# A Fourier and SwiGLU block: seven second products per weight group in place of eight, another modulation sum and a finer handing out

## The chip, the cores and the metric

One core of a Trainium2 chip. The metric is device time in microseconds (us) of one execution; lower is better. The engines are TensorE (PE, matmuls, with its weight loads PEld), VectorE (DVE), ScalarE (ACT), GpSimd (POOL) and the DMA queues, which SyncE (SP) and POOL feed here.

## The reference

The shapes are x: (1, 2048, 512), w1 and w3: (512, 1792), w2: (1792, 512), w_mod: (512, 3072), all fp32.

```
mod = (silu(c) @ w_mod).reshape(1, 6, 1, 512)
sa, ca, ga, sb, cb, gb = mod
h = layernorm(x) * (1 + ca) + sa
x = x + ga * fourier(h)              # real part of a 2-D DFT, by four DFT matrices
h = layernorm(x) * (1 + cb) + sb
x = x + gb * ((silu(h @ w1) * (h @ w3)) @ w2)
```

## The kernel before

**Precision.** Every fp32 operand is split in a high part (a rounded copy made on ACT) and a low part (the difference, made on DVE). A product is three matmul passes: high-high, high-low, low-high (`PASSES`, `product` L98). One matmul is 128 x 128 against 128 x 512.

**Stages.** Hidden-dimension DFT (to about 88 us in the profile), sequence DFT (to 262), then the SwiGLU part. The sequence stage also works off a queue of background steps: the columns of w_mod for ga, sb, cb and gb (`mod_columns` L344, multiply by silu(c) and sum along the row), and the second layernorm (`ln2` L817).

**SwiGLU.** The 2048 tokens are four chunks t = 0 to 3 of 512 columns, in pairs (0, 2) and (1, 3). The 1792 features are seven groups g of 256. Groups 0 and 1 of pair 0 are multiplied plainly: `up_block` for w1 and w3 (24 matmuls), then `down_unit` for w2. The order there is up(0,0), up(1,0), eight down units of chunk 0, then up(0,2), up(1,2), with up(g, t).

All else runs in twelve **items** (g, pair), counted 0 to 11: five of pair 0, then seven of pair 1, in `items`. In an item the first products are by Strassen's scheme (Winograd's form): seven products in place of eight block products for w1, called a1 to a7, and seven for w3, b1 to b7 (`factor` L1239). Each is a **unit** of six matmuls. ACT or DVE reads a unit's PSUM bank out, after which a later unit adds onto the same bank. DVE forms v = silu(gate) * up in `result` and v is split into hf. The second products, by w2, are units of six matmuls too, written **y**: eight an item, two chunks times four blocks of output columns, alternating on banks 6 and 7. ACT copies a bank into a tile y, scaled by gb (L335), and POOL adds two of them at a time onto `sums` in DRAM by an accumulating DMA. Items 10 and 11 (g = 5, 6 of pair 1) add on DVE onto reloaded sums `xr` instead. The y units of an item run inside the next item.

**Order.** The order on PE is written out by hand, as a string per item (last lines of `folded`): `-b7 a1 a2 -b4 -b3` (the leading minus is the last item's), then `a6 a5 y a7 y y a4 y a3 y b1 y b2 y b6 b5 y`. Item 5, the **turning** item (0, 1), has its own string. The weights of the next item, and this item's w2, are split by **jobs** (`weight_jobs` L1164: highs, sums, lows, highs and lows of the sums; `plain_jobs` for w2). Jobs and background steps are taken from their queues by `advance` after each unit or block, as long as a credit of DVE and ACT time lasts; each step declares its cost, and a `PAUSE` ends a call. `behind(n, f)` records f after n more units. Every engine runs its instructions in recorded order.

Of the kernel before, what the change touches and what calls it, by code (L numbers as in the profile page):

```python
# [42 lines left out]
def folded(nc, pools, c, cp, wmr, wmc, x, xt, ctr, cti, wdr, wdi, w1, w3, w2, out):  # L43
# [300 lines left out]
    def mod_columns(v, dst):  # L344
        w = {}

        def fetch(i):
            w[i] = take(F32, "wmc")
            nc.sync.dma_start(w[i], wmc[v, i])

        def scale(i):
            times(w[i], w[i], sc_row[0][:, 0, :].unsqueeze(1).to_broadcast([P, 2, N]))

        def total(i):
            r1 = small.tile([P, 32], F32, name=f"r1_{v}_{i}", tag="r1")
            nc.vector.tensor_reduce(
                out=r1,
                in_=flat(w[i]).rearrange("p (a b) -> p a b", b=32),
                axis=AX.X,
                op=OP.add,  # L360
            )
            nc.vector.tensor_reduce(
                out=dst[:, 2 * i : 2 * i + 2],
                in_=r1.rearrange("p (a b) -> p a b", b=16),
                axis=AX.X,
                op=OP.add,
            )
            give(w[i])
# [12 lines left out]
        background.extend([PAUSE] * 2)  # L381
        for i in range(2):
            step(background, 0, lambda i=i: scale(i), 1.2)
            step(background, 0, lambda i=i: total(i), 1.3)
        step(background, 0, end, 0.1)


# [685 lines left out]
            later[n - 1] = later.pop(n)  # L1073


    def up_block(g, t, q, w):
        if q == 0 and w == "w1":
            drain(lambda: ("h2", t, 1) in done)
        to = bank(turn[0] % 4)
        turn[0] += 1  # L1080
        for d in range(ND):
            at = slice(d * P, (d + 1) * P)
            product(
                to,
                [u[:, q, at] for u in wuse[w, g]],
                [u[t, d // 2][:, d % 2, :] for u in (h2h, h2l)],
                d == 0,
                d == ND - 1,
            )
        if t == PAIRS[0][1] and q == 1:  # L1090
# [117 lines left out]
    TO = {1: 0, 6: 0, 7: 0, 4: 0, 2: 1, 5: 2, 3: 2}  # L1208
    state, vs = {}, {}

    def right(pair, n):
        t0, t1 = PAIRS[pair]
        if n in (1, 2, 3):
            at = {1: (t0, 0), 2: (t0, 1), 3: (t1, 1)}[n]
            return h2h[at], h2l[at]
        at = pair, {5: 1, 6: 2, 7: 3, 4: 4}[n]
        return th[at], tl[at]

    def result(i, w, q, k, src):
# [6 lines left out]
        times(v, v, src)  # L1226

        def highs():
            hf[g, PAIRS[pair][k], q] = take(F32R, "hf")
# [5 lines left out]

        behind(1, highs)
        behind(2, lows)

    def factor(i, w, n):  # L1239
        g, pair = items[i]  # L1240
# [36 lines left out]
        if n == 3:  # L1277
            for x in wuse.pop(key).values():
                give(x)
            behind(1, lambda: give(st["x"]))  # L1280
            if w == "w3":
                for x in vs.pop(i):
                    behind(3, lambda x=x: give(x))


    loads.extend((n, m) for n in range(len(steps)) for m in range(2))
# [292 lines left out]
    def down(g, pair, t, d, key):  # L1579
        drain(lambda: (key, "l") in done, jobs)  # L1580
        delayed()
        down_unit(g, pair, t, d, key)
        beside(1.36, USED["own" if pair == 1 and g >= NG - 2 else "y"])

    for w in ("w1", "w3"):
# [25 lines left out]
    def other_operands():  # L1611
# [6 lines left out]
                give(h.pop((0, n)))  # L1618
        sum_parts(jobs, *sums_of.pop())

    def unit(kind, i, n):
        g, pair = items[i]
        more = i + 1 < len(items)
# [14 lines left out]
        if (kind, n) == ("a", 3) and more:  # L1638
            load_w(("w3", *items[i + 1]))
            weight_jobs(i + 1, "w1")  # L1640
        if (kind, n) == ("b", 2):
            plain_jobs(("w2", g, pair))
        if (kind, n) == ("b", 3):
            if i + 2 == turning:
                drain(lambda: ("xc", 3) in done)
# [7 lines left out]
            for t in PAIRS[pair]:  # L1653
                seconds.extend((g, pair, t, d, ("w2", g, pair)) for d in range(ND))
        beside(1.36, FACTOR[kind][n])

    weight_jobs(0, "w3")
# [822 lines left out]
```

## Time and profile before

| | us |
|---|---|
| median of 3 runs | 708.48 (707.67 to 708.64) |
| the profiled execution | 708.46 |
| its span, first to last instruction | 706.7 |
| up and down stage, 262 to 320: PE, DVE, ACT busy | 55.72, 43.34, 32.69 of 58 |
| items 0 to 4, 320 to 470: PE, DVE, ACT busy | 148.43, 130.02, 105.25 of 150 |
| item 5, 470 to 500: PE, DVE, ACT busy | 30.00, 20.47, 20.51 of 30 |
| the end, 650 to 706.7: PE, DVE, ACT busy | 48.55, 31.80, 15.02 of 56.7 |

A matmul's duration in the profile (0.39) is longer than its share of PE, since matmuls overlap; the distance between two starts is what a matmul costs. The same holds for ACT and DVE instructions that follow each other without a wait. A wait is shown in square brackets with the engine and the tile that ended it.

### The profile page before, as it was taken

The page shows a single profiled execution, that of the slowest core. Times are in us where ns is not written, and L with a number is a line of the kernel's source. Part 1 is how long each engine was busy: PE and PEld are TensorE (multiplying, and loading weights), DVE is VectorE, ACT ScalarE, POOL GpSimd, SP SyncE. Part 2 cuts the span into 40 slices and gives each one's busy share as a digit, 9 for nine tenths or more (in the row PEclk, how much of TensorE's full clock was granted, in tenths as well). Part 3 has the DMA queues.
Part 4 walks back from the last instruction along what each step waited for, and adds up shares of the span by engine and source line. Part 5 has one row for each costly group of instructions (what it writes and reads, how often), then busy time and mean ns, then how long its engine had stood idle before and what let it go on. Part 6 is the DMA issues. An engine that isn't in the chain of part 4 may idle for free.

```text
span 706.7 us, 8912 instructions
## 1 busy us (share of the span) xinstructions
PE 686.3 (97%) x3152; PEld 564.7 (80%) x3152; DVE 548.3 (78%) x877; ACT 430.8 (61%) x709; POOL 119.4 (17%) x141
## 2 busy tenths in 40 slices
PE   7999999999999999899999999999999999999995
PEld 4898888888888888687888788787788888888784
DVE  5999679997999978579987886896865556664763
ACT  4998865545454655745677676867665565656420
POOL 1320253542524000200100101011010100101000
PEclk9999999999999999999999999999999999999998
DMA  8730299796678521522868558376763847537403
GB/s 266 211 120 1 77 373 328 251 307 229 207 283 287 168 86 41 92 58 64 209 114 199 89 130 153 61 156 137 239 136 73 180 62 175 111 69 162 137 0 124
DMA packets 38100, 108.93 MB, mean 154 GB/s; under 512 B 4896, under 2 KB 5152, under 8 KB 38048
## 3 DMA queue, kind: packets, MB, share of 16 engines
q0 software_dynamic: 12352, 43.00, 29.3%
q1 hardware_dynamic: 25264, 63.98, 27.5%
q10 hardware_dynamic: 432, 1.31, 0.5%
q8 instruction: 26, 0.43, 0.3%
q14 instruction: 26, 0.21, 0.1%
HBM read 76.81 MB, written 33.55 MB: 156 GB/s over the span
## 4 chain that ended last, share of the span: by engine, by line
PE 81%; DVE 7%; ACT 6%; issue 2%; DMA 2%; SPq 1%; ACTq 0%; DVEq 0%
PE bank L100 52%; PE bank L750 25%; PE bank L559 2%; PE bank L598 1%; DMA wmr<-in_wmr 1%; ACT xc L894 1%; PE bank L576 1%; DVE xc L96 1%; SPq L231 1%; ACT hf L87 1%; ACT y L335 1%; DVE v L96 0%; DVE hl L90 0%; ACT hm L501 0%; DMA w<-in_wdi 0%
## 5 line engine op out<-in xcount | busy, mean ns | idle before, releaser
L100 PE MATMUL bank<-hf,w2h 128*128 128x512 f32 (+1 forms) x452 | 140.9, 391 | 0.3
L1146 POOL DMA_DIRECT2D sum<-y x48 | 41.0, 855 | 390.1 <-ACT y L335 373.0
L100 PEld LDWEIGHTS bank<-hf,w2h 128*128 128x128 f32 x452 | 84.3, 188 | 22.1 <-DVE hf L90 3.4
L100 PE MATMUL bank<-hf,w2l 128*128 128x512 f32 (+1 forms) x226 | 87.6, 388 | 0.0
L87 ACT ACTIVATE hf<-v 128x512 fp32r<-128x512 f32 x56 | 35.3, 630 | 67.3 <-DVE v L96 62.7
L335 ACT ACTIVATE y<-bank,gb 128x512 f32<-128x512 f32 x96 | 64.9, 682 | 18.6 <-PE bank L100 18.3
L93 DVE TENSOR_TENSOR v<-bank,x 128x512 f32<-128x512 f32 x36 | 24.7, 685 | 34.9 <-PE bank L100 34.8
L750 PE MATMUL bank<-bh,us 128*128 128x512 f32 x128 | 49.9, 390 | 0.0
L93 DVE TENSOR_TENSOR x<-bank,x 128x512 f32<-128x512 f32 x36 | 24.7, 687 | 32.4 <-PE bank L100 28.7
L750 PE MATMUL bank<-bh,ul 128*128 128x512 f32 x128 | 49.8, 389 | 0.0
L750 PE MATMUL bank<-d,us 128*128 128x512 f32 x128 | 49.8, 389 | 0.0
L750 PE MATMUL bank<-d,uh 128*128 128x512 f32 x128 | 49.8, 389 | 0.0
L750 PE MATMUL bank<-l,us 128*128 128x512 f32 x128 | 49.8, 389 | 0.0
L750 PE MATMUL bank<-l,uh 128*128 128x512 f32 x128 | 49.8, 389 | 0.0
L100 PEld LDWEIGHTS bank<-hf,w2l 128*128 128x128 f32 x226 | 42.4, 188 | 8.4
L90 DVE TENSOR_TENSOR hf<-v,hf 128x512 fp32r<-128x512 f32 x56 | 38.5, 687 | 12.2 <-ACT hf L87 12.1
L170 POOL DMA_INDIRECT re<-in_ctr,mirror x32 | 35.8, 1117 | 66.2 <-DVE ul L90 39.5
L1224 ACT ACTIVATE v<-v 128x512 f32<-128x512 f32 x36 | 22.8, 632 | 38.8 <-DVE v L93 38.8
L87 ACT ACTIVATE x<-bank 128x512 f32<-128x512 f32 x72 | 41.4, 586 | 7.2 <-PE bank L100 6.5
L170 POOL DMA_INDIRECT im<-in_cti,mirror x32 | 32.7, 1023 | 35.3 <-PE bank L750 10.0
L100 PE MATMUL bank<-h2h,w1h 128*128 128x512 f32 x80 | 31.8, 397 | 1.5 <-ACT h2h L87 1.5
L100 PE MATMUL bank<-h2l,w1h 128*128 128x512 f32 x80 | 31.9, 399 | 0.8 <-DVE h2l L90 0.8
(246 smaller groups left out, 1775.2 us busy)
## 6 DMA issues: line engine op xcount, KB each, us to landing
sum<-y POOLq DMA_DIRECT2D x48, 512.0 KB, 5.6
w<-in_w SPq DMA_DIRECT2D x42, 512.0 KB, 4.5
re<-in_ctr SPq DMA_DIRECT2D x32, 256.0 KB, 5.0
im<-in_cti SPq DMA_DIRECT2D x32, 256.0 KB, 5.0
wmc<-in_wmc SPq DMA_DIRECT2D x8, 512.0 KB, 6.3
xr<-in_xt SPq DMA_DIRECT2D x8, 512.0 KB, 7.6
sum<-xr SPq DMA_DIRECT2D x8, 512.0 KB, 6.2
x<-in_x SPq DMA_DIRECT2D x11, 256.0 KB, 4.8
```

The costliest lines, as they stand in the source:

```text
L87: nc.scalar.activation(dst, src, AF.Copy, scale=scale)
L90: nc.vector.tensor_tensor(out=dst, in0=a, in1=b, op=OP.subtract)
L93: nc.vector.tensor_tensor(out=dst, in0=a, in1=b, op=OP.add)
L96: nc.vector.tensor_tensor(out=dst, in0=a, in1=b, op=OP.mult)
L100: nc.tensor.matmul(acc, lhs[a], rhs[b], start=first and n == 0, stop=last and n == len(PASSES) - 1, skip_group_check=more,)
L170: nc.gpsimd.indirect_dma_start(dst, None, rows, bass.IndirectOffsetOnAxis(ap=at, axis=0))
L231: queue.dma_start(raw_w[dt][q * 64 : (q + 1) * 64, m, :], w[i][par::2, q])
L335: nc.scalar.activation(dst, src, AF.Identity, scale=by)
L559: nc.tensor.matmul(halves(hb[k])[:, m, :], sides((hh, hl)[a][k])[:, dt, m, :], wu[dt][:, b, m, :], start=False, stop=dt % 2 == 1 and n == ...
L750: nc.tensor.matmul(acc[what, e], lhs, rhs, start=begin and i == 0, stop=(end or (turn and what == "x")) and i == len(terms) - 1, skip_grou ...
L1146: nc.gpsimd.dma_start(sums[t, d // 2], y, accum_op=OP.add)
L1224: behind(k != 0 or q == 0, lambda: nc.scalar.activation(v, src, AF.Silu))
```

## The change

**Second products.** For items 5 to 9, (0, 1) to (4, 1), listed in `SEVEN`, w2 is multiplied by seven products (`seven_unit`) in the order 2 5 3 1 6 7 4. Each is one unit: three matmuls on bank 6 and three on bank 7, half the output columns each. Products 2, 5 and 1 start the two banks anew; 3 adds onto 5, and 6, 7, 4 onto 1. After each, ACT copies both banks into a y tile and POOL accumulates it, seven times an item. `seven_parts` forms the seven right-hand operands from v (four differences on DVE and seven splits), `seven_jobs` the sums of w2 and their splits. The y strings of items 6 to 10 lose one y, and no two y follow each other directly.

**Weights.** In these items the job for the next w3 is queued at b6 and no longer at b3, except in item 5, where w3 stays at b3 and the w2 job moves from b2 to b3.

**Modulation.** The product and row sum of a w_mod tile (one multiply and two reductions of up to 1024 columns) become eight multiply-and-sum instructions of 128 columns and one small reduction. The declared cost is 2 x 0.9 for a tile, before 1.2 + 1.3.

**Handing out.** `up_block` runs in two halves, and `advance` is called after each with 1.36, before once with 2.72.

```diff
+        def total(i, b):
+            sums, junk = parts[i], w[i][:, b, :]
+            for n in range(ND):
+                nc.vector.scalar_tensor_tensor(
+                    junk[:, cols(n)],
+                    junk[:, cols(n)],
+                    1.0,
+                    sc_row[0][:, 0, cols(n)],
+                    op0=OP.mult,
+                    op1=OP.mult,
+                    accum_out=sums[:, b, n : n + 1],
+                )
...
-            step(background, 0, lambda i=i: scale(i), 1.2)
-            step(background, 0, lambda i=i: total(i), 1.3)
+            for b in range(2):
+                step(background, 0, lambda i=i, b=b: total(i, b), 0.9)
...
+    def seven_parts(i, q, k):
...
+        if (q, k) != (0, 1):
+            n = {(0, 0): 1, (1, 0): 2, (1, 1): 3}[q, k]
+            behind(1, lambda: high(n, v[q, k]))
+            behind(2, lambda: low(n, v[q, k]))
+            return
+        t1, t2, t3, t4 = v[0, 0], v[1, 1], v[0, 1], v[1, 0]
+        behind(1, lambda: minus(t1, v[0, 1], v[0, 0]))
+        behind(2, lambda: high(5, t1))
+        behind(2, lambda: minus(t3, v[1, 1], v[0, 1]))
+        behind(3, lambda: low(5, t1))
+        behind(3, lambda: minus(t2, v[1, 1], t1))
...
+    def seven_jobs(key):
...
+        step(jobs, 1, highs, 0.0, 1.0)
+        step(jobs, 1, totals, 1.4)
+        step(jobs, 1, lows, 1.2)
+        step(jobs, 1, sum_highs, 0.0, 1.0)
+        step(jobs, 1, sum_lows, 1.2)
+
+    def seven_unit(g, pair, n, key):
...
+        for e, to in enumerate(banks7):
+            at = int(LEFT7[n][1]) * HALF + e * P
+            product(
+                to,
+                [flat(wuse[key][x])[:, at : at + P] for x in names],
+                [u[:, b, :] for b in range(2)],
+                new,
+                True,
+                not new,
+            )
+            d = 2 * which + e
+            copy_by(y[:, e, :], to, gb[:, d : d + 1])
+        give(u)
+        nc.gpsimd.dma_start(sums[t, which], y, accum_op=OP.add)
+        behind(4, lambda: give(y))
+        if n == ORDER7[-1]:
...
+            if g == NG - 3:
+                for t in PAIRS[pair]:
+                    load_sums(t)
...
-                up_block(g, t, q, w)
-                beside(2.72, USED[w])
+                for part in range(2):
+                    up_block(g, t, q, w, part)
+                    beside(1.36, USED[w] if part else (0.0, 0.0))
...
-        if (kind, n) == ("b", 2):
-            plain_jobs(("w2", g, pair))
+        if (kind, n) == ("b", 3 if i == turning else 2):
+            (seven_jobs if (g, pair) in SEVEN else plain_jobs)(("w2", g, pair))
...
-            if more:
+            if more and not early_w3(i):
                 weight_jobs(i + 1, "w3")
...
+        if (kind, n) == ("b", 6) and more and early_w3(i):
+            weight_jobs(i + 1, "w3")
...
+        if i and items[i - 1] in SEVEN:
+            body = "a6 a5 a7 y a4 y a3 y b1 y b2 y b6 y b5 y"
```

Where the order moves, first on ACT, in the down units between up(1,0) and up(0,2). The tiles xc are chunk 2 after its layernorm, scaled in place; h2h is its high part, which up(0,2) reads; y are the copies of the eight units. Before:

```order
L335 ACTIVATE y_381_2743<-bank4_382_2744,gb_152 128x512
L335 ACTIVATE y_381_2743<-bank5_383_2759,gb_152 128x512
L335 ACTIVATE y_384_2769<-bank6_385_2770,gb_152 128x512
L894 ACTIVATE xc_348_2564<-xc_348_2564,sb_150,cb1_151 128x512 x2
L335 ACTIVATE y_384_2769<-bank7_386_2780,gb_152 128x512
L335 ACTIVATE y_387_2790<-bank4_388_2791,gb_152 128x512
L894 ACTIVATE xc_360_2611<-xc_360_2611,sb_150,cb1_151 128x512 x2
L335 ACTIVATE y_387_2790<-bank5_389_2801,gb_152 128x512
L335 ACTIVATE y_390_2810<-bank6_391_2811,gb_152 128x512
L87 ACTIVATE h2h_392_2819<-xc_348_2564 128x1024
L335 ACTIVATE y_390_2810<-bank7_394_2823,gb_152 128x512
L87 ACTIVATE h2h_395_2832<-xc_360_2611 128x1024
```

And in the changed kernel, at the same place:

```order
L897 ACTIVATE xc_342_2546<-xc_342_2546,sb_150,cb1_151 128x512 x2
L87 ACTIVATE hf_379_2797<-v_377_2777 128x512
L897 ACTIVATE xc_350_2616<-xc_350_2616,sb_150,cb1_151 128x512 x2
L335 ACTIVATE y_381_2804<-bank4_382_2805,gb_152 128x512
L335 ACTIVATE y_381_2804<-bank5_383_2813,gb_152 128x512
L87 ACTIVATE h2h_384_2822<-xc_342_2546 128x1024
L335 ACTIVATE y_386_2826<-bank6_387_2827,gb_152 128x512
L87 ACTIVATE h2h_388_2835<-xc_350_2616 128x1024
L335 ACTIVATE y_386_2826<-bank7_390_2839,gb_152 128x512
L335 ACTIVATE y_391_2849<-bank4_392_2850,gb_152 128x512
```

The scalings moved ahead of the first y copy, and both h2h from behind the seventh and eighth y copy to behind the second and third.

Second, on DVE in the head of item 6, from the product of b3 to the addition that reads a7's bank 0 (the last row); x, v and hf are item 5's results and their splits, w3s, w3l, w3sl and w2s, w2l, w2sl the sums and low parts of weights. Before:

```order
L96 TENSOR_TENSOR v_660_4327<-v_660_4327,x_695_4499 128x512
L93 TENSOR_TENSOR w3s_717_4617<-w3_700_4539 128x256
L90 TENSOR_TENSOR w3s_717_4617<-w3s_717_4617,w3_700_4539 128x256
L90 TENSOR_TENSOR w3s_717_4617<-w3_700_4539 128x256
L90 TENSOR_TENSOR w3s_717_4617<-w3_700_4539,w3s_717_4617 128x256
L90 TENSOR_TENSOR hf_715_4605<-v_661_4328,hf_715_4605 128x512
L90 TENSOR_TENSOR w3l_720_4634<-w3_700_4539,w3h_716_4615 128x1024
L90 TENSOR_TENSOR hf_718_4623<-v_660_4327,hf_718_4623 128x512
L90 TENSOR_TENSOR w3sl_724_4648<-w3s_717_4617,w3sh_721_4636 128x1024
L93 TENSOR_TENSOR v_712_4584<-bank0_709_4575,x_723_4646 128x512
```

In the changed kernel, from the second sum on:

```order
L90 TENSOR_TENSOR w2s_715_4661<-w2s_715_4661,w2_687_4492 128x256
L90 TENSOR_TENSOR w2s_715_4661<-w2_687_4492 128x256
L90 TENSOR_TENSOR w2s_715_4661<-w2_687_4492,w2s_715_4661 128x256
L90 TENSOR_TENSOR hf_713_4649<-v_661_4376,hf_713_4649 128x512
L90 TENSOR_TENSOR v_660_4375<-v_660_4375 128x512
L90 TENSOR_TENSOR w2l_717_4677<-w2_687_4492,w2h_714_4659 128x1024
L90 TENSOR_TENSOR v_660_4375<-v_661_4376,v_660_4375 128x512
L90 TENSOR_TENSOR w2sl_722_4693<-w2s_715_4661,w2sh_718_4679 128x1024
L90 TENSOR_TENSOR hf_719_4681<-v_660_4375,hf_719_4681 128x512
L90 TENSOR_TENSOR v_661_4376<-v_661_4376,v_660_4375 128x512
L93 TENSOR_TENSOR v_710_4628<-bank0_707_4619,x_721_4691 128x512
```

w2's sums and low parts stand where w3's stood, w3's moved behind the addition, and three differences t1, t3, t2 (v from v) came in between.

Third, on ACT in items 7 to 9, from the copies of the fourth y on; x are copies of b units, w2h, w2sh and w3h high parts of weights. Before, from the copy ahead of w2h to the last y of the item:

```order
L335 ACTIVATE y_820_5190<-bank7_827_5214,gb_152 128x512
L87 ACTIVATE w2h_829_5232<-w2_805_5104 128x1024
L87 ACTIVATE hf_831_5236<-v_797_5055 128x512
L335 ACTIVATE y_832_5238<-bank6_833_5239,gb_152 128x512
L87 ACTIVATE x_825_5210<-bank3_824_5203 128x512
L87 ACTIVATE x_835_5262<-bank5_834_5255 128x512
L335 ACTIVATE y_832_5238<-bank7_836_5264,gb_152 128x512
```

And in the changed kernel, up to the copies of y6:

```order
L335 ACTIVATE y_848_5327<-bank7_847_5326,gb_152 128x512
L87 ACTIVATE w2h_850_5346<-w2_824_5218 128x1024
L87 ACTIVATE hf_852_5353<-v_819_5177 128x512
L335 ACTIVATE y_853_5355<-bank6_846_5325,gb_152 128x512
L335 ACTIVATE y_853_5355<-bank7_847_5326,gb_152 128x512
L87 ACTIVATE w2sh_855_5367<-w2s_851_5348 128x1024
L87 ACTIVATE x_844_5321<-bank3_843_5314 128x512
L87 ACTIVATE w3h_857_5379<-w3_837_5289 128x1024
L335 ACTIVATE y_858_5381<-bank6_846_5325,gb_152 128x512
L335 ACTIVATE y_858_5381<-bank7_847_5326,gb_152 128x512
```

Five y copies stand where three stood, with w2sh and w3h between them.

More of the change, by code (lines that the diff above doesn't have):

```diff
@@ L349, in fetch @@
             nc.sync.dma_start(w[i], wmc[v, i])
[L351 to L368, printed above, removed]
+        def total(i, b):
[10 more added lines that the diff above has]
+                )
+            if b:
+                nc.vector.tensor_reduce(
+                    out=dst[:, 2 * i : 2 * i + 2], in_=sums, axis=AX.X, op=OP.add
+                )
+                give(w[i])
+        parts = [
+            small.tile([P, 2, ND], F32, name=f"r1_{v}_{i}", tag="r1") for i in range(2)
+        ]
         def end():
@@ L1073, in delayed, with up_block @@
             later[n - 1] = later.pop(n)
-    def up_block(g, t, q, w):
-        if q == 0 and w == "w1":
+    def up_block(g, t, q, w, part):
+        if q == 0 and w == "w1" and part == 0:
             drain(lambda: ("h2", t, 1) in done)
-        to = bank(turn[0] % 4)
-        turn[0] += 1
-        for d in range(ND):
+        if part == 0:
+            cur["to"] = bank(turn[0] % 4)
+            turn[0] += 1
+        to = cur["to"]
+        for d in range(2 * part, 2 * part + 2):
             at = slice(d * P, (d + 1) * P)
@@ L1089, in up_block @@
             )
+        if part == 0:
+            return
         if t == PAIRS[0][1] and q == 1:
@@ L1619, in other_operands, with early_w3 @@
         sum_parts(jobs, *sums_of.pop())
+    def early_w3(i):
+        return items[i] in SEVEN and i != turning
     def unit(kind, i, n):
```

76 lines of the change are left out of this document (71 added, 5 removed).

## The prediction

> **What bounds the kernel now.** I read the page's busy table first, then busy time by stretches, then the matmuls in order of time around each place where TensorE (PE) stops, then ScalarE (ACT) and VectorE (DVE) in order of time within one item of the second half. Times are us from the span's start. A stretch's line has its length and then, busy us and instructions, PE, weight loads, DVE, ACT and POOL.
>
> ```profile
> PE 686.3 (97%) x3152; PEld 564.7 (80%) x3152; DVE 548.3 (78%) x877; ACT 430.8 (61%) x709; POOL 119.4 (17%) x141
> PE 81%; DVE 7%; ACT 6%; issue 2%; DMA 2%; SPq 1%; ACTq 0%; DVEq 0%
> 88.00:262.00 174.00, 174.00 (x769) 143.95 (x769) 157.09 (x220) 92.48 (x178) 60.27 (x59) 1.00 0.75 255
> 500.00:650.00 150.00, 149.79 (x656) 122.27 (x655) 92.84 (x142) 91.76 (x136) 16.19 (x19) 1.00 0.58 125
> ```
>
> PE is the bound nearly everywhere: 174.00 of 174 us in the sequence stage and 149.79 of 150 in the items where the change works. In these items DVE (92.84 of 150) and ACT (91.76) have a third of their time free; in the sequence stage DVE has little (157.09 of 174). So removed matmuls shorten the run only while DVE and ACT keep up.
>
> ```profile
> 558.05 0.39 PE L100 MATMUL bank<-th,w3sh 128*128 128x512 f32 x1
> 559.41 0.39 PE L100 MATMUL bank<-th,w3sh 128*128 128x512 f32 x1
> 409.84 0.39 PE L100 MATMUL bank<-h2h,w1h 128*128 128x512 f32 x1
> 440.01 0.40 PE L100 MATMUL bank<-h2h,w1h 128*128 128x512 f32 x1
> ```
>
> A unit of six matmuls starts 1.36 us after the one before it, 0.2267 us a matmul. An item (22 units, 29.9 us) takes 30.17 from its a1 to the next a1.
>
> The one large hole is where the second token chunk starts, before the items:
>
> ```profile
> 294.80 0.39 PE L100 MATMUL bank<-hf,w2l 128*128 128x512 f32 x1
> 296.71 0.51 PE L100 MATMUL bank<-h2h,w1h 128*128 128x512 f32 x1 [1.53 <-ACT h2h L87]
> 297.97 0.79 PE L100 MATMUL bank<-h2l,w1h 128*128 128x512 f32 x1 [0.76 <-DVE h2l L90]
> 300.27 0.63 PE L100 MATMUL bank<-h2h,w1h 128*128 128x512 f32 x1
> 300.70 0.50 PE L100 MATMUL bank<-h2l,w1h 128*128 128x512 f32 x1
> 301.03 0.39 PE L100 MATMUL bank<-h2h,w1l 128*128 128x512 f32 x1
> ```
>
> PE waits 1.53 for the high part of the normalised chunk and 0.76 for its low part, and then runs some matmuls 0.43 apart instead of 0.23. The matmul at 301.03 is the ninth after 294.80; at full pace it stood at 294.80 + 9 x 0.2267 = 296.84. The hole costs 4.2.
>
> **The change part by part.** The sum is made on the profiled execution: 708.46, of which 706.7 is span and 1.8 lies around it; the median is 708.48, so the two can be used alike.
>
> (1) Matmuls. A second product took 8 units an item and takes 7 in the five items (0,1) to (4,1): 30 matmuls less, 30 x 0.2267 = **6.8 saved**.
>
> (2) The handing out. The modulation sums are declared at 16 x 0.9 us in place of 8 x 2.5, and a block hands out steps twice, passing twice the pauses. So the second normalisation moves forward: its Sqrt stands in the first up block of group 1, no longer behind the second down unit, and both h2h of chunk 2 stand five y copies earlier on ACT. The hole of **4.2 goes**. What is late next is on ACT: all four xc scalings now stand ahead of the first y copy.
>
> ```profile
> 285.78 1.28 ACT L880 ACT_TABLE_LOAD   x1
> 290.49 1.53 ACT L894 ACTIVATE xc<-xc,sb,cb 128x512 f32<-128x512 f32 x2 [1.37 <-issue]
> ```
>
> The two table loads of 1.28 and two scalings of 1.53 bring the bank-4 copy to about 6.5 us after the down units start, by adding the rows on ACT and DVE from the last Silu on; the fifth unit wants that bank at 5.4. I add back **1.6** (0 to 3, with the slow matmuls that such a wait brings). Queued behind this copy are the other y copies and both h2h; the second low part is then ready at about 11.0 and wanted at 12.5.
>
> (3) The later normalisations, chunks 1 and 3, are handed out earlier too and no longer fall into the heads of items, where they held the x copies and the v additions:
>
> ```profile
> PE bank L100 <- ACT x L87: 1.0, 2, 0.5
> 450.76 0.50 PE L100 MATMUL bank<-th,w1sh 128*128 128x512 f32 x1 [0.48 <-ACT x L87]
> 455.43 0.50 PE L100 MATMUL bank<-th,w1h 128*128 128x512 f32 x1 [0.27 <-DVE v L93]
> ```
>
> 1.0 and 0.3 of waits; by the spacing of the matmuls around them, some 0.1 more for each restart and 0.4 ahead of each of the two longer ones, they cost **2.1, saved** (0 to 3).
>
> (4) The added work on DVE and ACT. The pitch in a full queue, not the duration, is what counts:
>
> ```profile
> 565.22 0.63 ACT L87 ACTIVATE hf<-v 128x512 fp32r<-128x512 f32 x1 [2.19 <-DVE v L96]
> 565.75 0.58 ACT L87 ACTIVATE x<-bank 128x512 f32<-128x512 f32 x1
> 572.11 1.06 ACT L87 ACTIVATE w3sh<-w3s 128x1024 fp32r<-128x1024 f32 x1 [0.41 <-DVE w3s L90]
> 573.08 0.58 ACT L87 ACTIVATE x<-bank 128x512 f32<-128x512 f32 x1
> 573.55 0.68 ACT L335 ACTIVATE y<-bank,gb 128x512 f32<-128x512 f32 x1
> 580.26 0.69 ACT L335 ACTIVATE y<-bank,gb 128x512 f32<-128x512 f32 x1 [0.76 <-PE bank L100]
> 580.85 1.05 ACT L87 ACTIVATE w1h<-w 128x1024 fp32r<-128x1024 f32 x1
> ```
>
> hf 0.53, a weight 0.97, x 0.47, y 0.59 (Silu taken as hf). Per item ACT gains 6 y, 3 hf and 1 weight: 6 x 0.59 + 3 x 0.53 + 0.97 = 6.1.
>
> ```profile
> 569.13 0.69 DVE L93 TENSOR_TENSOR x<-bank,x 128x512 f32<-128x512 f32 x1 [0.67 <-PE bank L100]
> 571.27 0.42 DVE L90 TENSOR_TENSOR w3s<-w 128x256 f32<-128x256 f32 x1
> 571.60 0.42 DVE L90 TENSOR_TENSOR w3s<-w,w3s 128x256 f32<-128x256 f32 x1
> 573.67 0.68 DVE L90 TENSOR_TENSOR hf<-v,hf 128x512 fp32r<-128x512 f32 x1
> 574.28 1.22 DVE L90 TENSOR_TENSOR w3sl<-w3s,w3sh 128x1024 fp32r<-128x1024 f32 x1
> 575.41 0.68 DVE L93 TENSOR_TENSOR v<-bank,x 128x512 f32<-128x512 f32 x1
> ```
>
> DVE: 0.34 for 256 columns, 0.61 for 512, 1.13 for 1024. Per item 7 of 512, 4 of 256 and one of 1024 are added: 4.3 + 1.4 + 1.1 = 6.8. Both engines fit into an item on average (before, 92.8/150 x 30.2 = 18.7 and 18.5). What matters is where the queue is long when PE wants a bank.
>
> *The first item with such products (item 6).* The head puts two sets of jobs at b3: w2 with its sums, which y1 needs, and w3. From the end of b3, DVE does the addition of b3 and its product (0.2 + 0.73 + 0.61), four sums of w2 (1.43), hf, t1, w2l, t3, w2sl, hf, t2 (5 x 0.61 + 2 x 1.13), then the addition of a7 (0.69): 9.0 us. PE wants bank 0 for a4 after a6 a5 a7 y1, 5.4 us. The same sum for the old order gives 7.1, and the rows show it: from 569.13 to the end of the addition at 575.41 + 0.68 = 576.09 are 6.96. There PE had six units, 8.2, to cover it. So a4 is **3.5 late** (0.9 of it already in y1, which waits for w2l). Behind the late addition stand the Silu of a7 and then y1's copies on ACT; followed to the item's end this gives 0.8 at y3 and 0.9 at y7. After the long wait matmuls run slow as at 297.97, where 4.2 - 1.53 - 0.76 = 1.9 of the hole is not waiting; most of that falls into later waits, and I add 0.5 (0 to 1.9). **5.7 in all** (3.5 to 7.5).
>
> *Items 7 to 9.* Without weights in the head the same sum is 5.3 us and a4 is on time. ACT is then full: from the Silu of a7 (12.3 after b7 began) to y6's first copy stand 3 Silu, 10 y, 3 hf, 5 weights, 2 x and that copy, 1.6 + 5.9 + 1.6 + 4.9 + 0.9 + 0.7 = 15.6, with 0.4 of waiting for v: 28.3. y7 adds onto that bank and would start at 27.2. A wait of about 1 us an item, **2.9** for three (0 to 6). Item 10 has no w2 sums and no late w3: 0.3.
>
> (5) Modulation itself. The small multiply-and-sum of 128 columns isn't in the trace; its bounds are 0.2 (the line through 256 and 512 columns above) and 0.74 (this row, 512 columns):
>
> ```profile
> L96 DVE TENSOR_TENSOR wmc<-wmc,scr x8: 1217/1218/1245, 108.9 to 184.6; 128x1024 f32<-128x1024 f32 x8
> L356 DVE TENSOR_REDUCE r<-wmc x8: 1220/1220/1221, 110.2 to 185.8; 128x32 f32<-128x1024 f32 x8
> L805 DVE SCALAR_TENSOR_TENSOR xr<-sum,ga,xr x16: 743/746/747, 190.3 to 334.3; 128x512 f32<-128x512 f32 x16
> ```
>
> I take 0.27, nearer the 256-column row: 64 x 0.27 = 17.3 against 8 x 2.44 = 19.5. On the path 0, because PE covers DVE in this stage (157 of 174). At 0.74 it is 47 us, 28 more than before: DVE would need 185 of 174, and PE would lose some 11. [...]
>
> (6) Accumulating DMAs, 7 an item for 4.
>
> ```profile
> q0 software_dynamic: 2636, 9.61, 40.4%
> q1 hardware_dynamic: 2675, 9.08, 17.7%
> sum<-y POOLq DMA_DIRECT2D x19, 512.0 KB, 5.8
> w<-in_w SPq DMA_DIRECT2D x14, 512.0 KB, 5.9
> ```
>
> In 150 us: 0.404 x 150 / 19 = 3.2 of all queues each, loads 0.177 x 150 / 17 = 1.6. An item: 7 x 3.2 + 3 x 1.6 = 27 of 29.8. It fits; a y buffer is written again some 20 tiles later, so the delay stays behind other work. Only the reload of the sums for the last items, behind y7, may be late: **0.3**. Without that cover each late accumulate costs up to 3.2.
>
> Sum: -6.8 - 4.2 + 1.6 - 2.1 + 5.7 + 2.9 + 0.3 + 0.3 = -2.3, **706.2**.
>
> **Rivals.** (A) The queues keep up: PE never waits in items 6 to 10 beyond item 6's 3.5. For it: a third of DVE and ACT is free. Against: the sums in (4). 708.5 - 6.8 - 4.2 + 1.6 - 2.1 + 3.5 = 700.5.
> (B) The saving is eaten: waits in the upper half of their bounds (6.7 in item 6, 4.5 in the next three), 708.8, no change. For it: DVE and ACT would be busy (18.7 + 6.8) and (18.5 + 6.1) of 29.8, 86 and 83%; against: most waits then have cover.
> (C) Slower, at the ACT queue of items 6 to 9: the overlap of 0.1 us that separates duration from pitch is lost whenever an instruction waits. With 24 instructions from Silu to y6, each 0.05 lost is 1.2 per item, 4.8 in four, so from 0.024 on nothing is left of the gain and from 0.04 on the loss can be told; at 0.05 it ends at 711.0, at 0.1 at 715.8. For it: every y copy waits for PE, every hf for DVE. Against: the rows of (4) overlap between unlike instructions.
> (D) The change doesn't clear the hole at 295 since the chunk is still late: 706.2 + 2.6 = 708.8, inside (B)'s result. The new order on ACT speaks against it.
> [...]
>
> **How the numbers follow.** The forecast, 702.5 to 707, has 0.41; (A), below that, 0.16; (B) and (D), 707 to 710, 0.18; (C) 0.25. About 0.2%, 1.4 us, can be told from no change: faster 0.57, same 0.18, slower 0.25. The range leaves out the lower part of (A) and the upper of (C): 700 to 711.5; the forecast's own is 702.5 to 707.
>
> **What would show it.** 30 matmuls fewer and an a1-to-a1 distance of 29.5 to 30.0 in items 7 to 9; PE waiting for ACT's y before y6 and y7; about 34 us for item 6, with PE waiting for DVE's v before a4; no wait for h2h near 295 and a short one for a y copy just before it; no wait at an a4 for xc work in items 0 to 4. It is wrong if items 7 to 9 exceed 30.2, if item 6 is under 32, or if the stage before 262 grows.

## The result, and the profile after

The change makes the kernel slower: 711.68 us (median of nine, 709.75 to 715.62) against 707.38 for the kernel before on the same chip (nine, 706.69 to 708.74); ratio 1.0067, interval 1.005 to 1.0085. The prediction was 706.2 with a range of 700 to 711.5.

Six of the nine times lie between 709.75 and 711.9, with a mean granted clock of 0.989 to 0.994, and three at 715.5 with 0.986. The profile is of one of the three (715.62, span 713.7). A second profile of the same kernel has a span of 710.0 (`whole_again` below). Both are used, since what only one of them has is no fixed part of the change.

From the first profile, the busy line of the page, then the chain that ended last:

```profile
PE 685.3 (96%) x3122; PEld 561.2 (79%) x3122; DVE 578.1 (81%) x1049; ACT 456.4 (64%) x759; POOL 134.6 (19%) x156
PE 71%; DVE 13%; ACT 7%; DMA 3%; issue 3%; SPq 1%; DVEq 0%; ACTq 0%
```

The chain now runs through DVE for 13% of the span, before for 7%. What PE waited for from the sequence stage on, in the view of waits (total us, times, longest; a row of 0.2 is left out):

```profile
PE bank L100 <- ACT y L335: 3.6, 6, 1.2
PE bank L100 <- DVE v L93: 2.3, 1, 2.3
PE bank L100 <- DVE v L96: 2.0, 1, 2.0
PE bank L100 <- ACT x L87: 1.3, 1, 1.3
PE bank L753 <- DVE xr L808: 0.9, 1, 0.9
PE bank L100 <- DVE w2l L90: 0.8, 1, 0.8
```

To see where these fall, the profiles are cut at matmuls that all kernels have: the last of the sequence stage, the first a6, and the a1 of items 1, 6, 7, 10 and 11. Lengths in us; "first" and "second" are the two profiles of the change:

| stretch | before | change, first profile | second | predicted difference | measured, first | second |
|---|---|---|---|---|---|---|
| to the end of the sequence stage | 262.15 | 263.31 | 263.21 | 0 | +1.2 | +1.1 |
| up and down stage, to the first a6 | 61.96 | 63.19 | 63.26 | -2.6 | +1.2 | +1.3 |
| first a6 to a1 of item 1 | 24.86 | 26.89 | 24.61 | in the next row | +2.0 | -0.3 |
| a1 of item 1 to a1 of item 6 | 153.64 | 151.50 | 151.48 | -2.1 | -2.1 | -2.2 |
| item 6 | 30.72 | 36.84 | 35.37 | +4.3 | +6.1 | +4.7 |
| items 7 to 9 | 90.50 | 89.89 | 89.88 | -1.2 | -0.6 | -0.6 |
| item 10 | 30.16 | 29.16 | 29.14 | -1.1 | -1.0 | -1.0 |
| item 11 and the end | 52.71 | 52.92 | 53.05 | +0.3 | +0.2 | +0.3 |
| sum | 706.7 | 713.7 | 710.0 | -2.4 | +7.0 | +3.3 |

Item 6 and all that follows came nearly as forecast. What did not is the second row, a gain of 2.6 that became a loss of 1.2, and what hangs on it in the third. The first row, 1.1 where 0 was forecast, is taken up under the modulation in the part on the prediction.

**A new stop at the head of the first item.** PE in the first profile, in order of time (start, duration, and in brackets the wait):

```profile
320.91 0.40 PE L100 MATMUL bank<-h2h,w1l 128*128 128x512 f32 x1
323.31 0.50 PE L100 MATMUL bank<-h2h,w1h 128*128 128x512 f32 x1 [2.00 <-DVE v L96]
326.50 0.80 PE L100 MATMUL bank<-th,w1sh 128*128 128x512 f32 x1 [1.33 <-ACT x L87]
327.09 0.63 PE L100 MATMUL bank<-tl,w1sh 128*128 128x512 f32 x1
```

The matmul at 323.31 opens a2 of the first item. It needs the bank of the sixth up block of the second chunk, free only when DVE has multiplied that block into v (the row of L96). DVE at that time:

```profile
318.84 1.22 DVE L90 TENSOR_TENSOR w1l<-w,w1h 128x1024 fp32r<-128x1024 f32 x1
320.11 1.23 DVE L90 TENSOR_TENSOR w1sl<-w1s,w1sh 128x1024 fp32r<-128x1024 f32 x1
321.25 1.41 DVE L808 SCALAR_TENSOR_TENSOR xr<-sum,ga,xr 128x512 f32<-128x512 f32 x2
322.58 0.68 DVE L96 TENSOR_TENSOR v<-v,bank 128x512 f32<-128x512 f32 x1
```

and DVE before the change, at the same instructions:

```profile
314.63 1.23 DVE L90 TENSOR_TENSOR w1l<-w,w1h 128x1024 fp32r<-128x1024 f32 x1 [0.34 <-ACT w1h L87]
315.77 0.68 DVE L96 TENSOR_TENSOR v<-v,bank 128x512 f32<-128x512 f32 x1
316.37 1.22 DVE L90 TENSOR_TENSOR w1sl<-w1s,w1sh 128x1024 fp32r<-128x1024 f32 x1
```

Before, the product stood ahead of w1sl; now w1sl and two residual sums (L808), handed out between the halves of the next block, stand ahead of it. By the spacing PE loses 2.2 here and 1.7 at a6, where it lost 0.4 before. The x copy that a6 waits for is queued on ACT behind the high part of the next late product:

```profile
325.34 0.63 ACT L87 ACTIVATE hf<-v 128x512 fp32r<-128x512 f32 x1 [0.86 <-DVE v L96]
325.87 0.58 ACT L87 ACTIVATE x<-bank 128x512 f32<-128x512 f32 x1
```

In the first profile a dozen matmuls at 0.43 instead of 0.2267 follow, 2.3 more; in the second profile none. Such matmuls are called slow below.

**Item 6**, PE, first profile:

```profile
516.36 0.50 PE L100 MATMUL bank<-hf,w2l 128*128 128x512 f32 x1 [0.79 <-DVE w2l L90]
519.90 0.80 PE L100 MATMUL bank<-th,w1h 128*128 128x512 f32 x1 [2.33 <-DVE v L93]
520.50 0.63 PE L100 MATMUL bank<-tl,w1h 128*128 128x512 f32 x1
```

The waits are the two that were forecast: y1 for w2l, then a4 for the addition of a7. By the spacing they cost 0.95 + 2.49 = 3.4, forecast 3.5; slow matmuls follow.

**Items 7 to 9.** PE, from the a1 of item 7 to the next:

```profile
541.73 0.39 PE L100 MATMUL bank<-h2h,w1h 128*128 128x512 f32 x1
568.83 0.73 PE L100 MATMUL bank<-hf,w2h 128*128 128x512 f32 x2 [0.49 <-ACT y L335]
571.69 0.39 PE L100 MATMUL bank<-h2h,w1h 128*128 128x512 f32 x1
```

571.69 - 541.73 = 29.96, 0.2 less than the 30.17 before, though 6 x 0.2267 = 1.36 of matmuls are gone. Product 4, the last y of the item (the row at 568.83), adds into the two banks of product 7 and waits for ACT to copy them.

**The modulation.** DVE from 88 to 262, one group of its instructions (count, busy us with overlaps counted once, mean ns), and then two of them in order of time:

```profile
L354 DVE SCALAR_TENSOR_TENSOR wmc<-wmc,scr 128x128 f32<-128x128 f32 x64 | 14.5, 287 | 0.0
```

```profile
125.97 0.29 DVE L354 SCALAR_TENSOR_TENSOR wmc<-wmc,scr 128x128 f32<-128x128 f32 x1
126.18 0.08 DVE L354 DVE_READ_ACCUMULATOR wmc<-wmc,scr 128x1 f32 x1
126.18 0.28 DVE L354 SCALAR_TENSOR_TENSOR wmc<-wmc,scr 128x128 f32<-128x128 f32 x1
```

Each multiply-and-sum is two records: the operation (0.28) and a read of the accumulator (0.08), which overlaps the next operation (both start at 126.18). From start to start it is 0.213 on average.

### The profile page after: what moved, and what is told of

Same layout as the page of the kernel before. It is cut to its first block, busy times and chain, and to the rows that moved or that the text cites. A ratio compares the mean times of both kernels' runs of the same rounds, so it can differ in the third digit from the quotient of the medians.

```text
span 713.7 us, 9124 instructions
## 1 busy us (share of the span) xinstructions
PE 685.3 (96%) x3122; PEld 561.2 (79%) x3122; DVE 578.1 (81%) x1049; ACT 456.4 (64%) x759; POOL 134.6 (19%) x156
## 4 chain that ended last, share of the span: by engine, by line
PE 71%; DVE 13%; ACT 7%; DMA 3%; issue 3%; SPq 1%; DVEq 0%; ACTq 0%
PE bank L100 48%; PE bank L753 18%; PE bank L562 2%; PE bank L601 1%; DMA wmc<-in_wmc 1%; ACT y L335 1%; DVE xr L808 1%; DVE v L96 1%; DMA w<-in_wdr 1%; DVE d L93 1%; DVE wmc L354 1%; DVE l L90 1%; PE bank L579 1%; DVE x L93 1%; DVE d L90 1%
## 5 line engine op out<-in xcount | busy, mean ns | idle before, releaser
L100 PE MATMUL bank<-hf,w2h 128*128 128x512 f32 (+1 forms) x352 | 109.4, 391 | 3.8 <-ACT y L335 3.6
L87 ACT ACTIVATE hf<-v 128x512 fp32r<-128x512 f32 x71 | 44.8, 631 | 75.9 <-DVE v L96 69.9
L335 ACT ACTIVATE y<-bank,gb 128x512 f32<-128x512 f32 x126 | 82.1, 688 | 11.8 <-PE bank L100 11.6
L100 PEld LDWEIGHTS bank<-hf,w2h 128*128 128x128 f32 x352 | 65.1, 188 | 21.8 <-ACT y L335 7.2
L1153 POOL DMA_DIRECT2D sum<-y x28 | 24.0, 857 | 247.8 <-ACT y L335 235.1
L100 PE MATMUL bank<-hf,w2l 128*128 128x512 f32 (+1 forms) x176 | 68.3, 388 | 0.8 <-DVE w2l L90 0.8
L90 DVE TENSOR_TENSOR hf<-v,hf 128x512 fp32r<-128x512 f32 x71 | 48.9, 689 | 17.5 <-ACT hf L87 17.3
L1345 POOL DMA_DIRECT2D sum<-y x35 | 29.8, 851 | 134.3 <-ACT y L335 129.5
L170 POOL DMA_INDIRECT im<-in_cti,mirror x32 | 36.4, 1138 | 29.7 <-issue 11.0
L100 PEld LDWEIGHTS bank<-hf,w2l 128*128 128x128 f32 x176 | 33.0, 188 | 7.9 <-DVE w2l L90 1.2
L100 PE MATMUL bank<-h2h,w1h 128*128 128x512 f32 x80 | 31.3, 391 | 2.0 <-DVE v L96 2.0
```

Of the source, the lines that this page charges most:

```text
L87: nc.scalar.activation(dst, src, AF.Copy, scale=scale)
L90: nc.vector.tensor_tensor(out=dst, in0=a, in1=b, op=OP.subtract)
L100: nc.tensor.matmul(acc, lhs[a], rhs[b], start=first and n == 0, stop=last and n == len(PASSES) - 1, skip_group_check=more,)
L170: nc.gpsimd.indirect_dma_start(dst, None, rows, bass.IndirectOffsetOnAxis(ap=at, axis=0))
L335: nc.scalar.activation(dst, src, AF.Identity, scale=by)
L1153: nc.gpsimd.dma_start(sums[t, d // 2], y, accum_op=OP.add)
```

## The experiments

Every kernel was timed against the kernel before on its own chip; ratios are to that. There were three groups of four. In the first two the kernel before had medians of 707.24 and 707.93, in the third 710.05. On that chip all four profiles, each of a changed kernel, show a stop of 1.4 to 1.7 early in the sequence stage, near 91, that no profile of the others has; the kernel before was not profiled there. Only ratios are compared between groups.

**The parts alone (first group).** In mod_only, blocks are whole again and `SEVEN` is empty (an extract; the w2 job of item 5 is back at b2 too):

```diff
-    SEVEN = [(g, 1) for g in range(NG - 2)]
+    SEVEN = []
-                for part in range(2):
-                    up_block(g, t, q, w, part)
-                    beside(1.36, USED[w] if part else (0.0, 0.0))
+                up_block(g, t, q, w)
+                beside(2.72, USED[w])
```

> Modulation by multiply-and-sum alone; whole blocks, eight products a second product in every item. My theory: the stop of the sequence stage near 132 (1.1) belongs to this part; the hole near 295 (1.53 and 0.76 of waits) goes, since the steps of the second chunk come earlier by this part alone, worth 2.8 net; the collisions in items 1 to 4 go (2.4); and the new stop near 323 (waits of 2.00 and 1.33) does not come, because in this order DVE still does the product of the block before w1sl and the residual sums. So 707.4 + 1.1 - 2.8 - 2.4 = 703.3. Rival: the stop near 323 belongs to the earlier normalisation, whichever part brings it forward: then it is here too, 703.3 + 6.2 = 709.5.

Measured 708.0; ratio 1.0004 (0.9993 to 1.0015). Neither theory held. The hole near 295 is gone and a2 doesn't wait, as my theory had it, but a6 waits 1.68 for ACT's x copy, and the collisions in the heads of two early items are still there (waits of 0.49 and 0.29 in each): the stretch from the a1 of item 1 to that of item 6 is 154.91, before 153.64. Nothing stopped near 132 in this profile.

half_only keeps the halves and has the old `scale` and `total` of the modulation and an empty `SEVEN`.

> Half-block handing out alone; modulation in two passes, eight products everywhere. My theory: no stop near 132, the hole near 295 goes (2.8 net), items 1 to 4 gain 2.4, and the stop near 323 comes, since w1sl and two residual sums stand ahead of the block's product on DVE: + 6.2. So 707.4 - 2.8 - 2.4 + 6.2 = 708.4. Rival (the stop comes of both parts together, that is of six residual sums in a row): no stop here, 702.2.

Measured 710.93; ratio 1.0045 (1.0027 to 1.0063). The halves alone bring the new stop: a2 waits 0.84 for DVE's product and a6 2.80 for x. The wait at a2 is theirs; one at a6 is in mod_only too, so that one is not theirs alone. The loss is larger than expected because the y copy ahead of it is later too, 1.79 instead of 1.17, with slow matmuls behind it. The collisions of items 1 to 4 are gone here: that they go is the halves' doing, not the modulation's.

seven_only has the old modulation and whole blocks.

> Seven products with the moved weight preparation alone. My theory: item 6 is 6.1 longer than before, items 7 to 9 together 0.6 and item 10 1.0 shorter, the last 0.2 longer, as in the profile of the whole change: 707.4 + 4.7 = 712.1. By the prediction's terms - 6.8 + 5.7 + 2.9 + 0.3 + 0.3 = + 2.4: 709.8. Rival (item 6 was only long because of what went before it in the whole change): at most 707.4.

Measured 712.23; ratio 1.0067 (1.0046 to 1.0089). Item 6 is 36.6 and items 7 to 9 are 29.9 each, as in the whole change, so this loss needs nothing of the other parts.

The three parts alone sum to 0.04 + 0.45 + 0.67 = 1.2%, the whole is 0.67 and, below, 0.8%. The parts do not simply add: halves and modulation each remove the same hole near 295, which by itself would make the sum too small, and each has a wait at the same a6 and the modulation alone the longer items 1 to 5, which make it too large.

> The whole change once more. Its nine times were 709.8 to 711.9 six times and 715.5 three times, and the profile is one of the three. My theory: the two groups differ by the slow matmuls after one of the two long waits (327 to 331.3, or 519.9 to 526.0); in a profile of the lower group one of them is missing, and each is worth 11 to 15 matmuls at 0.2 extra, 2 to 3. Rival: they differ by a wait itself, a transfer that lands later, or by the clock all over.

Measured 712.39 (711.19 to 715.23); ratio 1.008 (1.0048 to 1.0111). This profile has the same waits as the first. PE in it, at a6 of the first item and at a4 of item 6:

```profile
326.47 0.50 PE L100 MATMUL bank<-th,w1sh 128*128 128x512 f32 x1 [1.54 <-ACT x L87]
326.81 0.40 PE L100 MATMUL bank<-tl,w1sh 128*128 128x512 f32 x1
...
517.53 0.80 PE L100 MATMUL bank<-th,w1h 128*128 128x512 f32 x1 [2.34 <-DVE v L93]
518.13 0.63 PE L100 MATMUL bank<-tl,w1h 128*128 128x512 f32 x1
```

At a6 the next matmul follows 0.34 later and then at full pace; at a4 it takes 0.6 and about seven matmuls are slow, until 520.4 instead of 526.0 - 2.4 = 523.6 on the same scale. That is the first of the two theories in kind: the waits agree within 0.2, and the slow matmuls, all gone at a6 and half of them at a4, make up the 3.7 between the two spans.

**Each loss mended (second group).** chunk2_whole takes the halves from the second chunk:

```diff
                 for part in range(2):
                     up_block(g, t, q, w, part)
-                    beside(1.36, USED[w] if part else (0.0, 0.0))
+                    if t != 2:
+                        beside(1.36, USED[w] if part else (0.0, 0.0))
+                if t == 2:
+                    beside(2.72, USED[w])
```

> The whole change, but the blocks of the second token chunk hand out steps once, after both halves, so that DVE does the product of the last block but one ahead of w1sl and the residual sums. My theory: the stop near 323 is made of that order alone; its two waits go (2.16 and 1.70 in both profiles of the change) and with them the slow matmuls behind it where a run has them (2.3 in the first profile, none in the second): 712 - 3.9 to 712 - 6.2, 706 to 708, and no wait for DVE's v between 318 and 332 above 0.5. Rival: DVE simply has too much to do there (24.2 of 30 us before 320); then the wait moves one or two blocks on, and the time stays above 710.5.

Measured 708.63; ratio 0.9998 (0.9983 to 1.0012): a time equal to that of the kernel before, where the change was 0.67 and 0.8% slower. DVE, and PE at a6, in its profile:

```profile
317.33 1.22 DVE L90 TENSOR_TENSOR w1l<-w,w1h 128x1024 fp32r<-128x1024 f32 x1
318.46 0.68 DVE L96 TENSOR_TENSOR v<-v,bank 128x512 f32<-128x512 f32 x1
319.06 1.22 DVE L90 TENSOR_TENSOR w1sl<-w1s,w1sh 128x1024 fp32r<-128x1024 f32 x1
```

```profile
325.33 0.50 PE L100 MATMUL bank<-th,w1sh 128*128 128x512 f32 x1 [0.32 <-ACT x L87]
```

The product stands ahead of w1sl again, and the only wait left between 318 and 332 is 0.32. The up and down stage, to the first a6, is 59.33: 2.6 shorter than before, which is what was forecast for it, and 3.9 shorter than in the change. DVE is busy 25.0 of the 30 us from 290 to 320 here and 24.2 in the change, so the order of its work decides, not the amount; the rival falls. The sequence stage ended late in this profile, at 266.00, but that does not explain it: last_product_late ends it at 265.90 and has both waits (2.00 and 1.54), and all_three, with this edit, ends it at 262.15 and has 0.29 at a6 and none at a2.

from_group1 gives item 5 its eight products back and item 6 the old body:

```diff
-    SEVEN = [(g, 1) for g in range(NG - 2)]
+    SEVEN = [(g, 1) for g in range(1, NG - 2)]
-        if (kind, n) == ("b", 3 if i == turning else 2):
+        if (kind, n) == ("b", 2):
```

> The whole change, but seven products only in items 6 to 9, so that the item behind the turn has the old body and six units ahead of a4; six matmuls more. My theory: item 6 is 30.7 again instead of 35.4 and 36.8 in the two profiles, so 712 - 4.7 to 712 - 6.1, about 706.5. Rival: the w2 sums are late in the first item that has them, wherever it is: then item 7 is longer than 32 and the time above 709.

Measured 707.41; ratio 0.999 (0.9966 to 1.0013). The a1 of items 6 and 7 on PE:

```profile
501.65 0.39 PE L100 MATMUL bank<-h2h,w1h 128*128 128x512 f32 x1
532.37 0.39 PE L100 MATMUL bank<-h2h,w1h 128*128 128x512 f32 x1
```

Item 6 is 30.72, as before the change. Item 7 (532.37 to 562.67 by the next a1), now the first whose head follows new second products, is 30.30, with one wait of 0.23 at a4: where the w2 sums are made in the body of an item, they are not late.

last_product_late moves the seventh product one unit on:

```diff
-            body = "a6 a5 a7 y a4 y a3 y b1 y b2 y b6 y b5 y"
+            body = "a6 a5 a7 y a4 y a3 y b1 y b2 y b6 y b5"
...
+        if i > 1 and items[i - 2] in SEVEN:
+            head = "-b7 y a1 a2 -b4 -b3 "
```

> The whole change, but the seventh product of an item stands behind the next b7 instead of ahead of it. In the profile it waits 0.49 in each of items 6 to 10 for the two ACT copies of product 7, which adds into the same banks, and restarts slowly. My theory: this wait is 1.36 short of cover and goes: 0.64 an item, five items, 712 - 3.2 = 708.8. Rival: ACT is simply full there, and PE waits for the copy of the next unit (x or y) instead: 711 to 713.

Measured 709.28; ratio 1.0021 (1.0001 to 1.0042). PE, product 4, and two a1:

```profile
567.58 0.62 PE L100 MATMUL bank<-hf,w2h 128*128 128x512 f32 x2
...
568.94 0.39 PE L100 MATMUL bank<-h2h,w1h 128*128 128x512 f32 x1
...
598.10 0.39 PE L100 MATMUL bank<-h2h,w1h 128*128 128x512 f32 x1
```

The wait is gone and the item is 29.16, 0.8 shorter than in the change. In the change the wait stood in four items, 6 to 9, not in five; item 10 was 29.16 already. ACT is busy 90.75 us of the 120 between 542 and 662 in the change and 93.17 here, so over an item it was not full; only ahead of this wait does its queue run without a gap but one of 0.8, for 16.2 us. One unit more of cover was enough for that, and no later unit waits instead.

all_three has the three edits together.

> The three edits of this call together: whole blocks in the second chunk, seven products from group 1 on, the last product behind b7. If the three losses are apart from each other they add: 712 - 4.7 - 5.3 - 2.6 (four items) = 699.4, which is faster than before by 1.1%. If they only moved the same wait on, the best of them is what is left: 706 or more.

Measured 701.3 (700.69 to 702.42); ratio 0.9907 (0.989 to 0.9924), faster than both kernels. On the scale of 707.4 the ratio gives 700.8, 11.2 below 712, where the three would give 12.6 if they simply added. Its busy line, and PE's longest waits from the up stage on:

```profile
PE 679.2 (97%) x3128; PEld 558.7 (80%) x3128; DVE 569.8 (82%) x1037; ACT 450.3 (64%) x749; POOL 132.4 (19%) x153
```

```profile
PE bank L100 <- ACT y L335: 1.9, 3, 1.2
PE bank L100 <- ACT x L87: 0.3, 1, 0.3
PE bank L100 <- DVE v L93: 0.2, 1, 0.2
```

PE waits 2.4 in these rows, against 10.0 in the five rows of line L100 shown for the change; DVE is as busy as there (82 and 81%).

**What each part is worth once mended (third group).** seven_mended is the kernel before with the seven products from group 1 on and the last product late.

> The kernel before with only the seven products, mended in the two ways that helped (from group 1 on, the last product behind b7). In the run with all three edits the stretch from item 6 to item 11 is 147.67 against 151.38 before. My theory: that part stands alone, 707.4 - 3.7 = 703.7. Rival: it needs the earlier normalisation of the other two parts, and gains under 1 without: above 706.4.

Measured 706.56 against 710.05; ratio 0.9955 (0.9926 to 0.9984), by the ratio 3.2 us. The part stands alone; a gain under 1 would be a ratio above 0.9986, just outside the interval.

mended_without_modulation is all_three with the old `scale` and `total`.

> The run with all three edits, but with the old two-pass modulation. My theory: modulation alone was worth nothing (708.0 against 707.2), and the half blocks of the first chunk bring the normalisation forward without it: 701.3, within 1. Rival: the normalisation is early enough only with both; the hole near 295 is back: 701.3 + 2.5 = 703.8.

Measured 702.36; ratio 0.9887 (0.986 to 0.9914). The hole near 295 is not back; a wait of 1.80 for a y copy stands just before it. Its interval and that of all_three overlap: no worth of the new modulation can be told here.

mended_without_halves is all_three with whole blocks throughout.

> The run with all three edits, but with whole blocks throughout. By the run of modulation alone this is the mended seven products and nothing else: 703.7. By its profile (end 1.5 earlier than before, counted from the end of the sequence stage) 702.2. If the halves of the first chunk are what takes the collisions out of items 0 to 4, it is at least 1.5 slower than 701.3.

Measured 705.15; ratio 0.9926 (0.9898 to 0.9955), 702.1 on the scale of 707.4, the second of the expected numbers. The collisions in two early items are back in its profile (waits of 0.49 and about 0.3), so that gain is the halves', but the intervals overlap and its size in the time is not settled. At the first a6 it does not wait, though its instructions up to there are those of mod_only, which waits 1.68: its up stage begins 1.5 later, at 264.53, by the stop near 91, while DVE's last product of the second chunk starts at 320.11, in mod_only at 320.34. So the stop of this chip hides a wait that the order has.

**Filling the waits.** whole_filled adds matmuls that nothing reads where PE waits:

```diff
+        fill = {("a", 0, 2): (5, 8), ("a", 0, 6): (5, 6), ("a", turning + 1, 4): (4, 10)}
+        if (kind, i, n) in fill:
+            to, count = fill[kind, i, n]
+            idle = bank(to)
+            for _ in range(count):
+                nc.tensor.matmul(
+                    idle,
+                    flat(wuse["w1", g, pair]["h"])[:, :P],
+                    right(pair, 1)[0][:, 0, :],
+                    start=True,
+                    stop=True,
+                )
         factor(i, "w1" if kind == "a" else "w3", n)
```

> The whole change with 24 matmuls on ready operands that nothing reads, put on TensorE where it waits: 8 ahead of a2 and 6 ahead of a6 in the first item, 10 ahead of a4 in item 6. Theory: the slow matmuls (0.43 apart) that some executions show behind these waits come from TensorE having been idle; filled, none are left, the profile shows 0.2267 behind each of the three places, and the median falls from about 712 to 709 to 710. Rival: they come from the data or the state of the chip, whatever TensorE did before: 711 to 712 and slow matmuls behind the same places.

Measured 712.18 against 710.05; ratio 1.003 (1.0014 to 1.0046), 2.1 us slower than before, where the change unfilled is 1.0067 and 1.008. On the scale of 707.4 the ratio gives 709.5, as the theory had it; the time itself is nearer the rival's 711 to 712, on the chip where the kernel before is slower too. PE in its profile, at a2 of the first item and a4 of item 6:

```profile
321.66 2.01 PE L1761 MATMUL bank<-h2h,w1h 128*128 128x512 f32 x8
323.81 0.50 PE L100 MATMUL bank<-h2h,w1h 128*128 128x512 f32 x1
...
515.53 2.44 PE L1761 MATMUL bank<-h2h,w1h 128*128 128x512 f32 x10
518.04 0.50 PE L100 MATMUL bank<-th,w1h 128*128 128x512 f32 x1
```

The delays themselves remain (a4 starts as late as ever), and no matmul behind them is slow (0.23 apart from the second on). One profile can't show that they never are, since those of chunk2_whole and last_product_late, unfilled, have none behind a4 either. Eight of the ten executions have a mean granted clock of 0.993 to 0.996, higher than most of the change's (0.986 to 0.994), but two have 0.988, at 713.99 and 714.29. So the lower ratio speaks for the theory, and it is not settled.

## Why the prediction was wrong

- **Matmuls: right.** 30 fewer.
- **The hole near 295 goes, and a y copy is late instead: right.** The wait is 1.17 and costs 1.33; 1.6 was forecast.
- **"What is late next is on ACT": this step failed.** I followed the moved steps on ACT and DVE as far as the start of the second chunk, where the low part is in time, and stopped there. The steps handed out earlier stand in DVE's queue ahead of the products of the second chunk's blocks as well, and one of those holds the bank of the first item's a2. That is 2.2 + 1.7 = 3.9, where 0.4 was lost before, and up to 2.3 of slow matmuls, against nothing in the sum. chunk2_whole, which changes this order alone, takes the loss away and leaves the forecast gain of 2.6 in this stage; half_only, without the other parts, is 3.2 longer there than the kernel before. The order of DVE's instructions was there to be read, and no row of it was shown for this place.
- **Collisions in items 1 to 4: right**, -2.1 forecast, -2.1 and -2.2 measured. That the gain came from the halves and not from the modulation sums was left open in the prediction; the runs of the parts show it.
- **Item 6: right in mechanism and inside its bounds.** The cost, with the saved 1.36, is 6.0 and 7.5, forecast 5.7 (3.5 to 7.5). The two waits are 3.4 of 3.5; slow matmuls were taken as 0.5 and are 1.5 and 2.9 by their spacing. Of the waits placed at y3 (0.8) and y7 (0.9), the first did not come and the second, at the last product, was 0.5. The sum gives 30.7 + 4.3 = 35.0 for the item, where the signs said about 34; it is 36.8 and 35.4.
- **Items 7 to 9: mechanism right, size a little small.** The matmuls save 4.1, and 0.6 is left: 3.5 eaten, 2.9 forecast. The wait is the forecast one: the last y waits for ACT's copies of the y before it, at the end of a queue that was forecast at 16.0 us from the Silu of a7 on and took 16.2 (552.62 to 568.8 in the first profile). The rival with ACT's overlap lost, at its 0.05, would have made each item 0.8 longer than before, and they are 0.2 shorter.
- **Modulation on the path at 0: not settled.** Its 64 steps take 0.213 each from the start of one to the next, 13.6 in all instead of 19.5; I took 0.27. The 0.213 is near the 0.2 of the line through the plain rows, the lower of the two bounds. The sequence stage still ended 1.1 later in both profiles of the change, one of the signs of being wrong that I had named, with waits of 0.91 and 1.38 for residual sums near 132. The same stop is in chunk2_whole and last_product_late (0.3 to 0.4) and in seven_only, which has the old modulation (0.35), and not in mod_only, from_group1 or all_three. Up to there chunk2_whole, last_product_late, from_group1 and all_three have the instructions of the change. So with the same instructions the stop is anything from nothing to 1.38, and whether the modulation has a share in it stays open.
- **The chances.** 0.25 stood on slower, all of it on the ACT queue of items 6 to 9. Slower came, but by another cause. The rivals were looked for where the new work is, and none where old work had only been moved.

By the table's second profile, the sum of -2.4 misses 3.9 (to the first a6), 1.1 (sequence stage), 0.4 (item 6), 0.6 (items 7 to 9) and 0.1 (item 10), and gets 0.4 back from the first a6 to item 6: +3.3. The first profile adds 2.3 and 1.5 of slow matmuls.

## What to carry to other kernels

When a change hands steps out earlier, follow every queue that they enter to the next instruction that frees a bank or buffer for the bound engine, past the place that the change was aimed at. Here steps between two halves of a block stood ahead of the product of the block before, and cost 3.9 to 6.2 us where 4.2 - 1.3 = 2.9 had been gained. Count the units between a product and the next use of its bank: six matmuls fewer saved 0.2 us an item here as first written, and 1.0 with one product moved by one unit.

## What the hardware showed that was not expected

The same wait is sometimes followed by slow matmuls and sometimes not. At a4 of item 6 PE waits 2.33 or 2.34 in the two profiles of the change and in chunk2_whole, with 0.78 or 0.79 ahead of it; behind it about 14 matmuls are slow (0.43 apart) in the first, 7 in the second, none in chunk2_whole:

```profile
516.67 0.51 PE L100 MATMUL bank<-th,w1h 128*128 128x512 f32 x1 [2.34 <-DVE v L93]
```

The granted clock differs in the same way. The stretch from 512 to 528 in the three profiles (the third number from the end of a row is the mean granted clock):

```profile
512.00:528.00 16.00, 12.88 (x43) 9.76 (x42) 14.20 (x24) 10.99 (x18) 1.70 (x2) 0.79 0.35 68
512.00:528.00 16.00, 12.88 (x50) 9.93 (x49) 15.62 (x25) 13.58 (x22) 2.56 (x3) 0.89 0.46 70
512.00:528.00 16.00, 12.38 (x52) 9.34 (x51) 15.64 (x24) 13.91 (x22) 2.99 (x4) 1.00 0.49 78
```

Over the slow matmuls alone, 519.9 to 526.0 in the first profile, it is 0.50.

Behind a single wait of 1.79 in half_only matmuls are slow (0.43 apart), and behind one of 1.80 at the same place in mended_without_modulation they are not (0.23). The two rows on PE, of half_only:

```profile
291.19 0.73 PE L100 MATMUL bank<-hf,w2h 128*128 128x512 f32 x2 [1.79 <-ACT y L335]
...
292.95 1.06 PE L100 MATMUL bank<-hf,w2h 128*128 128x512 f32 x2
```

and of mended_without_modulation:

```profile
292.74 0.73 PE L100 MATMUL bank<-hf,w2h 128*128 128x512 f32 x2 [1.80 <-ACT y L335]
...
294.23 0.62 PE L100 MATMUL bank<-hf,w2h 128*128 128x512 f32 x2
```

No run here shows why the same wait has either outcome, and none varied the length of a wait alone, so a threshold isn't given. For reading times: the two profiles of the change differ by 3.7, and 2.3 + 1.5 of that are these slow matmuls.
